# An FFT filter and a squared-ReLU FFN in one kernel: W_in loaded in seven pieces, a reordered opening, two FFT stages one slot later, and x cast on GpSimd

## The chip, the cores and the metric

The kernel runs on one core of a Trainium2 chip. A core has five engines with queues of their own: TensorE (PE in the profile; its weight loads are PEld), VectorE (DVE), ScalarE (ACT), GpSimd (POOL) and SyncE (SP), which here only issues DMAs. TensorE reads the on-chip memory SBUF and writes the accumulator memory PSUM; VectorE and ScalarE copy results from PSUM to SBUF. The metric is the device time of one execution in microseconds (us). Before the change the median of 13 runs is 796.56 us, from 794.07 to 798.56.

## The reference

```python
def _attn_ref(x, filt_r, filt_i):              # x: (8, 3008, 256), filters: (1505, 256)
    X = np.fft.rfft(x, axis=1)
    F = (filt_r + 1j * filt_i)[None, :, :]
    Y = X * F
    return np.fft.irfft(Y, n=x.shape[1], axis=1).astype(np.float32)

def _moe_ref(x, w_in, w_out):                  # x: (24064, 256), w_in: (256, 2048), w_out: (2048, 256)
    h = np.maximum(x @ w_in, 0.0)
    return (h * h @ w_out).astype(np.float32)

out = _moe_ref(attn_out.reshape(8 * 3008, 256), w_in, w_out)
```

Each batch of x is filtered along its 3008 positions by a real FFT, a product with a complex filter, and the inverse transform. The 24064 rows that come out go through a two-layer FFN whose hidden values are rectified and squared. Inputs and output are float32; inside, the kernel works in float16 with float32 accumulation.

## The kernel before, in words

**The FFT as matmuls.** 3008 is 64 x 47, and the transform of a batch is done in four stages of matmuls with constant matrices. Stage A (`unit_a`; `chunk_a0` and `chunk_a` for batches 0 and 1) transforms along 47 and gives u. For batches 1 to 7, u is written to the DRAM buffer dU (`write_u`) and read back in another layout as ut (`read_u`); for batch 0 it is turned on TensorE (`turn_u`). Stage B (`unit_b`, 12 units a batch) transforms along 64 into psB; VectorE multiplies that by the filter sF (L451, "prod"), makes a swapped copy in two halves (L458, L459), and `unit_s` adds (L465). Stage P (`unit_p`, `unit_p0` for batch 0) goes back along 64, ScalarE copies the result to ze, and ze is written to the DRAM buffer dZ. `read_z` reads dZ back as four z tiles, and stage Y (`unit_y`, 16 units) goes back along 47; its result yt is copied by ScalarE (even units) or VectorE (odd units).

**The FFN.** 47 groups of 512 rows. `ffn_g1` (L560) makes 2 of 16 hidden tiles in one call, ScalarE rectifies them (L564), `ffn_sq` squares them on VectorE (L568), and `ffn_g2` (L577) multiplies by W_out; ScalarE copies the output (L588) and SyncE writes it.

**Slots.** All is unrolled, in an order written out by hand. The main loop at the end of the kernel runs over slots, 8 to a group: in each, g1 of the present group, the FFT units planned for "place 0", g2 of the group before, the units for "place 1", the output, and the square. `fft_plan(b)` puts each unit of batch b at a slot counted from a start of its own: slot 48 is that of the first group which needs rows of batch b (slot 40 for batch 1). Loads and casts of the next batch's x (`load_x`, `cast_x`) are in the plan too. Engines work through their own queues in program order; a DMA is issued by SyncE once what it waits for is done, and one that waits holds those behind it. Each engine waits for another only where data or a buffer demands it.

**Buffers.** A tile pool with a tag has so many buffers, and a new tile waits until the last use of the tile that had its buffer. Of the 32-bit tiles "x32" (1 MB) there are two; the opening uses them in turn for x of batch 0, for the two halves of W_in, and for x of batch 1. PSUM has two buffers each of psF, psO and psH; in the main loop stages A, B, P and Y share the two psF, g1 has psH and g2 has psO.

**The opening** (all before the main loop). It loads x of batch 0 as three tiles (`load_wide`), the filters (`load_f`), the constants, W_in and x of batch 1; casts them to float16 (`cast_wide`, `cast_win`, L680, L695); runs stage A of batch 0 and the turns; and spreads the filter into sF by small selection matmuls (`place_f(im, k)`: im is 0 for the real and 1 for the imaginary part, k counts groups of four columns; each call has about 0.87 us of matmuls and one copy of 1024 elements, L303 on ScalarE or L307 on VectorE). `sSPx` is a copy of the stage-P constants with the halves of the partitions swapped, made on GpSimd. Then a loop of seven rounds runs stages B and P of batch 0 with the rest of `place_f` between them:

```python
for k in range(7):
    if k < 6:
        unit_b(0, 2 * k)
        if k < 5:
            place_f(1, k + 1, nc.scalar)
        unit_b(0, 2 * k + 1)
    if k > 0:
        unit_p0(k - 1)
    if k < 2:
        place_f(0, k + 4, nc.scalar)
    if k in (1, 2):
        load_wide(1, k - 1)
        cast_wide(1, k - 1, nc.gpsimd, nc.gpsimd)
```

After it come the first reads of z and the load of W_out, stage A of batch 1 (`chunk_a`, lines 378 and 380), four Y units of batch 0, and slot 0. The product of unit p in stage B needs both `place_f(0, p // 2)` and `place_f(1, p // 2)`.

Of the kernel before, what the change touches and what calls it, by code (L numbers as in the profile page):

```python
# [110 lines left out]
def kernel(  # L111
# [96 lines left out]
    sPF = p_out.tile([128, 6, 128], F16, tag="ost", name="sPF")  # L208

    xw32, xw16 = {}, {}  # L210
    halves, later = ((0, 0), (0, 1)), []

    def load_wide(b, k):

        v0 = xrows[b * S:b * S + 2048, :].rearrange("(p m) d -> p m d", m=16)
        v1 = xrows[b * S + 2048:b * S + 3072, :].rearrange("(p m) d -> p m d", m=8)
        pool, tag = (p_x32, "x32") if k < 2 else (p_y, "yt") if b else (p_h2, "h2")
        t = pool.tile([128, 8, D], F32, tag=tag, name=f"xw_{b}_{k}")
        v = (v0[:, 0:8, :], v1, v0[:, 8:16, :])[k]
        for m in (slice(0, 4), slice(4, 8)) if (b, k) in halves else (slice(0, 8),):  # L220
            if m.stop > 4 and m.start == 4:
                later.append((t, v, m))
            else:
                nc.sync.dma_start(out=t[:, m, :], in_=v[:, m, :])
        xw32[(b, k)] = t

    def cast_wide(b, k, *engs, parts=(0, 1)):
        if 0 in parts:
            xw16[(b, k)] = p_x16.tile([128, 8, D], F16, tag="x16", name=f"xw16_{b}_{k}")
        for i in parts:  # L230
            m = slice(4 * i, 4 * i + 4)
            engs[i].tensor_copy(out=xw16[(b, k)][:, m, :], in_=xw32[(b, k)][:, m, :])
# [42 lines left out]

    f16s = []

    def place_f(im, k, eng, rotate=False):

        if rotate:  # L280
            banks, groups = bank_pair(f"psf_{im}_{k}")
        else:
            t = psH(f"psf_{im}_{k}")
            banks, groups = [t[:, 0, :], t[:, 1, :]], [(t, 0)]
        for i in range(4):
            c = 4 * k + i
            e0, e1 = D * c, D * (47 - c)
            cuts = [0] + [d for d in range(1, D)
                          if (e0 + d) % QF == 0 or (c and (e1 + d) % QF == 0)] + [D]
            for d0, d1 in zip(cuts, cuts[1:]):  # L290
                o = banks[i // 2][:, (i % 2) * D + d0:(i % 2) * D + d1]
                q, a = divmod(e0 + d0, QF)
                nc.tensor.matmul(o, sPF[:, PQ.index((0, q)), :], f16s[0][:, im, a:a + d1 - d0],  # L293
                                 start=True, stop=False)
                q, a = divmod(e1 + d0, QF) if c else (0, QF + d0)
                nc.tensor.matmul(o, sPF[:, PQ.index((1, q)), :], f16s[0][:, im, a:a + d1 - d0],  # L296
                                 start=False, stop=True)
        for t, i in groups:
            n = t.shape[1]
            dst = sF[:, im, 4 * k + 2 * i:4 * k + 2 * i + 2 * n, :]  # L300
# [21 lines left out]
    def load_wout(k):  # L322
        if k == 0:
# [9 lines left out]

    x16s, us, uts, prods, zes, zts, yts = {}, {}, {}, {}, {}, {}, {}

    def cast_x(b, c, eng=nc.vector):
        t = p_x16.tile([94, 8, D], F16, tag="x16", name=f"x16_{b}_{c}")
        eng.tensor_copy(out=t, in_=x32s.pop((b, c))[0:94])  # L338
        x16s[(b, c)] = t
# [49 lines left out]
                else:  # L389
                    eng.tensor_copy(out=o, in_=pv)  # L390

    def chunk_a0(c, ks):

        for k in ks:
# [213 lines left out]
    def fft_plan(b):  # L608
# [24 lines left out]
        if b + 1 < B:  # L633
            for c in range(2):
                put(t0 - 13, 1, load_x, b + 1, c)
            for c in range(4):
                r = t0 - 8 + 3 * c
                put(r, 1, cast_x, b + 1, c)
                if c < 2:
                    put(r, 1, load_x, b + 1, c + 2)  # L640
        for n in range(16):
            if b == 1:
                put(38 + n // 2 if n > 3 else 39, n % 2, unit_y, b, n)
            else:
                put(44 + n // 2, n % 2, unit_y, b, n)
        return plan

    def run(plan, r, place):
# [2 lines left out]


    uT = p_h2.tile([128, 2, NC, 128], F16, tag="h2", name="uT")
    for i in range(2):
        for k in range(2):
            cast_wide(0, k, nc.vector, nc.vector, parts=(i,))
    cast_wide(0, 2, nc.vector, nc.gpsimd)

    def load_const(t, d, k):
        c = slice(12 * k, 12 * k + 12)  # L660
# [11 lines left out]
    for k in range(2):  # L672
        for c in (1, 3):
            chunk_a0(c, (k,))
    f16s.append(p_h2.tile([128, 2, QF + D], F16, tag="h2", name="f16"))
    e0, e1 = slice(0, 1504), slice(1504, QF)
    for im in range(2):
        nc.gpsimd.tensor_copy(out=f16s[0][:, im, QF:], in_=nyq[:, im, :])
    for im, e in ((0, e0), (0, e1), (1, e0)):
        nc.gpsimd.tensor_copy(out=f16s[0][:, im, e], in_=f32s[im][:, e])  # L680
    for k in range(2):
        sSPx.append(p_u.tile([128, 12, 128], F16, tag="u", name=f"sSPx_{k}"))
        c = slice(12 * k, 12 * k + 12)
        nc.gpsimd.tensor_copy(out=sSPx[k][0:64], in_=sSP[64:128, c, :])
        nc.gpsimd.tensor_copy(out=sSPx[k][64:128], in_=sSP[0:64, c, :])
    for k in range(2):
        cast_win(k)
    uts[0] = p_ut.tile([128, NC, D], F16, tag="ut", name="ut_0")
# [24 lines left out]
    read_z(0, 1)  # L713
# [59 lines left out]
```

## Time and profile before

| what | value |
|---|---|
| median of 13 runs | 796.56 us (794.07 to 798.56) |
| the profiled execution | 796.39 us; span of its instructions 794.6 us |
| granted TensorE clock, mean | 0.997 |
| TensorE busy (PE) | 781.4 us, 98% of the span |
| VectorE, ScalarE, GpSimd busy | 552.4, 554.5 and 24.2 us |
| chain that ended last | PE 91%, DMA 5%, DVE 1%, ACT 1% |
| DMA | 107.32 MB, mean 135 GB/s |

The page follows one execution. A group line names the source line, the engine, the operation, out<-in, the shape and the count, then the group's busy time and the mean of one in ns, then the engine's idle time just before and who ended it. A timeline line gives the start and the length in us, the engine, the line, and the count of merged instructions; in square brackets stands the idle time before it and what ended it. Matmuls are pipelined, so the shown length of one is longer than the distance to the next: holes in TensorE are best read from the distances between starts.

### The profile page before, as it was taken

The page shows a single profiled execution, that of the slowest core. Times are in us where ns is not written, and L with a number is a line of the kernel's source. Part 1 is how long each engine was busy: PE and PEld are TensorE (multiplying, and loading weights), DVE is VectorE, ACT ScalarE, POOL GpSimd, SP SyncE. Part 2 cuts the span into 40 slices and gives each one's busy share as a digit, 9 for nine tenths or more (in the row PEclk, how much of TensorE's full clock was granted, in tenths as well). Part 3 has the DMA queues.
Part 4 walks back from the last instruction along what each step waited for, and adds up shares of the span by engine and source line. Part 5 has one row for each costly group of instructions (what it writes and reads, how often), then busy time and mean ns, then how long its engine had stood idle before and what let it go on. Part 6 is the DMA issues. An engine that isn't in the chain of part 4 may idle for free.

```text
span 794.6 us, 14801 instructions
## 1 busy us (share of the span) xinstructions
PE 781.4 (98%) x6102; PEld 553.1 (70%) x6102; DVE 552.4 (70%) x898; ACT 554.5 (70%) x708; POOL 24.2 (3%) x27
## 2 busy tenths in 40 slices
PE   8989999999999999999999999999999999999998
PEld 6746667667676667867677677776777667776666
DVE  6956995589755897559965699557995589554342
ACT  3866776767767676767777677676777767766664
POOL 3710000000000000000000000000000000000000
PEclk9999999999999999999999999999999999999999
DMA  9994554346714567155462555424663342511111
GB/s 350 369 272 137 149 148 126 90 138 165 204 42 111 163 159 179 41 172 148 125 168 59 162 153 149 117 73 154 155 177 91 90 141 80 125 45 41 40 41 54
DMA packets 88139, 107.32 MB, mean 135 GB/s; under 512 B 6288, under 2 KB 78864, under 8 KB 83856
## 3 DMA queue, kind: packets, MB, share of 16 engines
q1 hardware_dynamic: 87864, 106.19, 46.6%
q8 instruction: 48, 0.79, 0.4%
q10 hardware_dynamic: 144, 0.18, 0.1%
q14 instruction: 19, 0.16, 0.1%
q0 software_dynamic: 64, 0.00, 0.0%
HBM read 58.12 MB, written 48.23 MB: 134 GB/s over the span
## 4 chain that ended last, share of the span: by engine, by line
PE 91%; DMA 5%; DVE 1%; ACT 1%; SPq 0%; issue 0%; POOL 0%; ACTq 0%; DVEq 0%; POOLq 0%
PE psO L577 40%; PE psH L560 39%; PE psA L359 3%; PE psY L530 3%; PE psB L443 2%; PE psP L494 2%; DMA xw<-in_x_dram 2%; DMA ut<-dU 1%; DMA zt<-dZ 1%; PE psf L293 1%; ACT h L564 1%; PE psf L296 1%; ACT sF L303 0%; DMA dU<-u 0%; PE psT L420 0%; DMA dZ<-ze 0%
## 5 line engine op out<-in xcount | busy, mean ns | idle before, releaser
L564 ACT ACTIVATE h<-psH 128x1024 f16<-128x1024 f32 x376 | 384.9, 1024 | 190.4 <-PE psH L560 188.6
L577 PE MATMUL psO<-sWout,h 128*128 128x256 f16 x3008 | 388.6, 272 | 0.0
L560 PE MATMUL psH<-yt,sWin 128*128 128x512 f16 (+7 forms) x1728 | 386.9, 351 | 1.8 <-DVE yt L539 0.8
L577 PEld LDWEIGHTS <-h 128*128 128x128 f16 x3008 | 290.6, 98 | 77.2
L568 DVE TENSOR_TENSOR h<-h 128x1024 f16<-128x1024 f16 x376 | 253.8, 685 | 100.7 <-ACT h L564 99.2
L560 PEld LDWEIGHTS <-sWin 128*128 128x128 f16 x1728 | 159.5, 98 | 101.7 <-issue 3.5
L451 DVE TENSOR_TENSOR prod<-psB,sF 128x1024 f16<-128x1024 f32 x84 | 102.5, 1220 | 6.3 <-PE psB L443 6.0
L539 DVE CAST yt<-psY 128x376 f16<-128x376 f32 x62 | 34.0, 549 | 57.4 <-PE psY L530 57.4
L365 DVE CAST u<-psA 96x512 f16<-96x512 f32 x50 | 34.3, 687 | 47.3 <-PE psA L359 45.1
L496 ACT CAST ze<-psP 128x512 f16<-128x512 f32 x84 | 49.2, 585 | 17.9 <-PE psP L494 16.0
L588 ACT COPY ost<-psO 128x512 f32<-128x512 f32 (+1 forms) x96 | 55.8, 581 | 6.7 <-PE psO L577 5.3
L530 PEld LDWEIGHTS <-zt 112*128 112x128 f16 x512 | 34.8, 98 | 12.2 <-issue 2.3
L530 PE MATMUL psY<-sC,zt 112*128 112x94 f16 x512 | 42.3, 205 | 0.6 <-ACT yt L537 0.3
L465 DVE TENSOR_TENSOR yf<-prod,yf 128x512 f16<-128x512 f16 x84 | 35.7, 425 | 2.9
L443 PE MATMUL psB<-ut,sSB 128*128 128x256 f16 x192 | 36.5, 272 | 0.7 <-DMA ut<-dU 0.4
L359 PE MATMUL psA<-x,sC 94*96 94x512 f16 x96 | 36.6, 382 | 0.0
L443 PEld LDWEIGHTS <-sSB 128*128 128x128 f16 x192 | 18.6, 98 | 21.3 <-issue 2.2
L494 PE MATMUL psP<-yf,sSP 128*128 128x256 f16 x168 | 32.1, 273 | 0.2 <-ACT yt L537 0.2
L537 ACT CAST yt<-psY 128x376 f16<-128x376 f32 x66 | 30.8, 468 | 1.1 <-PE psY L530 0.6
L338 DVE CAST x<-x 94x2048 f16<-94x2048 f32 x24 | 29.2, 1216 | 0.0
L363 ACT CAST u<-psA 96x512 f16<-96x512 f32 x50 | 28.6, 572 | 0.0
L458 DVE COPY yf<-prod 64x512 f16<-64x512 f16 x84 | 24.3, 289 | 2.9
(63 smaller groups left out, 252.9 us busy)
## 6 DMA issues: line engine op xcount, KB each, us to landing
x<-in_x_dram SPq DMA_DIRECT2D x20, 768.0 KB
zt<-dZ SPq DMA_DIRECT2D x64, 192.0 KB
dU<-u SPq DMA_DIRECT2D x28, 384.0 KB
dZ<-ze SPq DMA_DIRECT2D x28, 384.0 KB
out_dram<-ost SPq DMA_DIRECT2D x66, 128.0 KB
out_dram<-ost SPq DMA_DIRECT2D x31, 256.0 KB
ut<-dU SPq DMA_DIRECT2D x7, 1024.0 KB
xw<-in_x_dram SPq DMA_DIRECT2D x4, 1024.0 KB
```

The source lines that it names most:

```text
L359: nc.tensor.matmul(ps[0:96, :], sSA, x16s[(b, c)][:, m, :], start=True, stop=True)
L443: nc.tensor.matmul(ps[:, i * D:(i + 1) * D], sSB[:, 2 * p + i, :], uts[b][:, 2 * p + i, :], start=True, stop=True)
L451: nc.vector.tensor_mul(out=prod, in0=ps.rearrange("p (a d) -> p a d", d=D).unsqueeze(1).to_broadcast([128, 2, 2, D]), in1=sF[:, :, 2 * p:2 ...
L465: nc.vector.tensor_add(out=yf, in0=prod[:, 0], in1=yf)
L494: nc.tensor.matmul(ps[:, i * D:(i + 1) * D], sSP[:, 2 * p + i, :], yf[:, i, :], start=True, stop=True)
L496: nc.scalar.copy(out=zes[(b, c)][:, 2 * i6:2 * i6 + 2, :], in_=ps.rearrange("p (a d) -> p a d", d=D))
L530: nc.tensor.matmul(ps[:, 94 * jj:94 * jj + 94], zt[:, 4 * (g % 2) + jj, dt * 128:(dt + 1) * 128], sSY, start=True, stop=True)
L560: nc.tensor.matmul(ps[:, i, o:o + n], sWin[:, dt, jt * 128:(jt + 1) * 128], yts[b][:, dt, r:r + n], start=(dt == 0), stop=(dt == 1))
L564: nc.scalar.activation(out=h2[:, 2 * s:2 * s + 2, :], in_=ps, func=AF.Relu)
L568: nc.vector.tensor_mul(out=v, in0=v, in1=v)
L577: nc.tensor.matmul(pso[g][:, t % 2, :], h2s[g][:, jt, t * 128:(t + 1) * 128], sWout[:, jt, :], start=(jt == 0), stop=(jt == NJT - 1))
L588: nc.scalar.copy(out=ost[:, h0:h0 + step, :], in_=pso[g][:, h0:h0 + step, :])
```

## The change

Three parts, done together.

- The opening. x of batch 0 is loaded in three whole tiles instead of the first two in halves. W_in is loaded in seven pieces into buffers of the tags ze, prod and yf, not into the two x32 buffers, and cast on GpSimd piece by piece. All three loads of batch 1's x are issued right after W_in's. The imaginary filter is cast in three parts on VectorE, GpSimd and ScalarE. `place_f(0, 2)` and `place_f(0, 3)` move from before the loop into it, and `place_f(1, 0)` may be split over two engines (it gets a PSUM tile of one piece, so ScalarE copies all of it). The sSPx copies are made in twelve pieces of 512 elements instead of four of 1536. The third x tile of batch 1 is cast on VectorE and ScalarE after the loop, no longer on GpSimd before it; the other two are cast on GpSimd after W_in.
- The plan. In batches 2 to 7, stage B begins at slot 19 (was 18) and ends at slot 37 as before, and Y takes slots 45 to 52 (was 44 to 51). In batch 1, stage B ends at slot 31 (was 32), z is read at slot 34 (was 35), and Y takes two units a slot from slot 38 (before, its first four units stood in slot 39). The loads of batch 2's x come one slot sooner.
- The x casts of batches 2 to 7 go from VectorE to GpSimd, one slot sooner in the plan (two in batch 1's); the loads of the third and fourth x tile are issued two slots after the cast whose buffer they take, not in its slot.

```diff
-    halves, later = ((0, 0), (0, 1)), []
...
-        for m in (slice(0, 4), slice(4, 8)) if (b, k) in halves else (slice(0, 8),):
-            if m.stop > 4 and m.start == 4:
-                later.append((t, v, m))
-            else:
-                nc.sync.dma_start(out=t[:, m, :], in_=v[:, m, :])
+        nc.sync.dma_start(out=t, in_=(v0[:, 0:8, :], v1, v0[:, 8:16, :])[k])
...
-    for k in range(2):
+    for k in range(3):
         load_wide(0, k)
-    for t, v, m in later:
-        nc.sync.dma_start(out=t[:, m, :], in_=v[:, m, :])
-    load_wide(0, 2)
...
-    def load_win(k):
-        w32s[k] = p_x32.tile([128, DFF], F32, tag="x32", name=f"win32_{k}")
-        nc.sync.dma_start(out=w32s[k], in_=moe_w_in[128 * k:128 * k + 128, :])
-
-    def cast_win(k):
-        for j in range(2):
-            c = slice(1024 * j, 1024 * j + 1024)
-            nc.gpsimd.tensor_copy(out=sWin[:, k, c], in_=w32s[k][:, c])
+    def load_win():
+
+        for k, c, n, pool, tag in ((0, 0, 768, p_ze, "ze"), (0, 768, 768, p_ze, "ze"),
+                                   (0, 1536, 512, p_prod, "prod"), (1, 0, 768, p_ze, "ze"),
+                                   (1, 768, 512, p_prod, "prod"), (1, 1280, 512, p_prod, "prod"),
+                                   (1, 1792, 256, p_yf, "yf")):
+            t = pool.tile([128, n], F32, tag=tag, name=f"win32_{k}_{c}")
+            nc.sync.dma_start(out=t, in_=moe_w_in[128 * k:128 * k + 128, c:c + n])
+            wins.append((t, k, slice(c, c + n)))
+
+    def cast_win():
+        for t, k, c in wins:
+            nc.gpsimd.tensor_copy(out=sWin[:, k, c], in_=t)
...
-    def cast_x(b, c, eng=nc.vector):
+    def cast_x(b, c, eng=nc.gpsimd):
...
-        t0 = 14 if b == 1 else 18
+        t0 = 14 if b == 1 else 19
         for p in range(12):
-            r = t0 + (18 if b == 1 else 19) * p // 11
+            r = t0 + (17 if b == 1 else 18) * p // 11
...
-        t0 = 35 if b == 1 else 40
+        t0 = 34 if b == 1 else 40
...
             for c in range(4):
-                r = t0 - 8 + 3 * c
+                r = t0 - 9 + 3 * c
                 put(r, 1, cast_x, b + 1, c)
                 if c < 2:
-                    put(r, 1, load_x, b + 1, c + 2)
+                    put(r + 2, 1, load_x, b + 1, c + 2)
         for n in range(16):
-            if b == 1:
-                put(38 + n // 2 if n > 3 else 39, n % 2, unit_y, b, n)
-            else:
-                put(44 + n // 2, n % 2, unit_y, b, n)
+            put((38 if b == 1 else 45) + n // 2, n % 2, unit_y, b, n)
...
-    for k in range(2):
-        load_win(k)
-    for k in range(2):
-        for c in (0, 2):
-            chunk_a0(c, (k,))
-    for k in range(2):
-        for c in (1, 3):
-            chunk_a0(c, (k,))
+    load_win()
+    for k in range(3):
+        load_wide(1, k)
+    for c in (0, 2, 1, 3):
+        chunk_a0(c)
...
-    for im, e in ((0, e0), (0, e1), (1, e0)):
-        nc.gpsimd.tensor_copy(out=f16s[0][:, im, e], in_=f32s[im][:, e])
+    for e in (e0, e1):
+        nc.gpsimd.tensor_copy(out=f16s[0][:, 0, e], in_=f32s[0][:, e])
+    uts[0] = p_ut.tile([128, NC, D], F16, tag="ut", name="ut_0")
+    turn_u(0, nc.scalar)
+    turn_u(1, nc.vector)
+    turn_u(2, nc.scalar)
+    turn_u(3, nc.vector)
+    place_f(0, 0, nc.scalar, rotate=True)
+    for eng, e in ((nc.vector, slice(0, 1024)), (nc.gpsimd, slice(1024, 2048)),
+                   (nc.scalar, slice(2048, QF))):
+        cast(eng, f16s[0][:, 1, e], f32s[1][:, e])
+    turn_u(4, nc.vector)
+    place_f(0, 1, nc.scalar, rotate=True)
+    turn_u(5, nc.vector)
+    place_f(1, 0, nc.scalar, nc.vector, rotate=True)
+    for k in range(6):
+        if k % 3 == 0:
+            sSPx.append(p_u.tile([128, 12, 128], F16, tag="u", name=f"sSPx_{k}"))
+        c, o = slice(4 * k, 4 * k + 4), slice(4 * k % 12, 4 * k % 12 + 4)
+        nc.gpsimd.tensor_copy(out=sSPx[-1][0:64, o, :], in_=sSP[64:128, c, :])
+        nc.gpsimd.tensor_copy(out=sSPx[-1][64:128, o, :], in_=sSP[0:64, c, :])
+    cast_win()
     for k in range(2):
...
-    load_wide(1, 2)
-    cast_wide(1, 2, nc.gpsimd, nc.gpsimd)
-    for k in range(6):
-        turn_u(k, nc.vector if k in (1, 3, 4, 5) else nc.scalar)
-        if k > 2:
-            place_f(0, k - 3, nc.scalar, True)
-    nc.vector.tensor_copy(out=f16s[0][:, 1, e1], in_=f32s[1][:, e1])
-    place_f(0, 3, nc.vector, True)
-    place_f(1, 0, nc.scalar)
+        cast_wide(1, k, nc.gpsimd, nc.gpsimd)
...
-        if k < 2:
-            place_f(0, k + 4, nc.scalar)
-        if k in (1, 2):
-            load_wide(1, k - 1)
-            cast_wide(1, k - 1, nc.gpsimd, nc.gpsimd)
+        if k < 4:
+            place_f(0, k + 2, nc.scalar)
+    cast_wide(1, 2, nc.vector, nc.scalar)
     read_z(0, 0)
```

More of the change, by code (lines that the diff above doesn't have):

```diff
@@ L218, in load_wide, with cast, cast_wide @@
         t = pool.tile([128, 8, D], F32, tag=tag, name=f"xw_{b}_{k}")
-        v = (v0[:, 0:8, :], v1, v0[:, 8:16, :])[k]
-        for m in (slice(0, 4), slice(4, 8)) if (b, k) in halves else (slice(0, 8),):
-            if m.stop > 4 and m.start == 4:
-                later.append((t, v, m))
-            else:
-                nc.sync.dma_start(out=t[:, m, :], in_=v[:, m, :])
-        xw32[(b, k)] = t
[L227 to L230, printed above, removed]
+        nc.sync.dma_start(out=t, in_=(v0[:, 0:8, :], v1, v0[:, 8:16, :])[k])
+        xw32[(b, k)] = t
+    def cast(eng, out, in_):
+        (eng.copy if eng is nc.scalar else eng.tensor_copy)(out=out, in_=in_)
+    def cast_wide(b, k, *engs):
+        t = p_x16.tile([128, 8, D], F16, tag="x16", name=f"xw16_{b}_{k}")
+        for i in range(2):
             m = slice(4 * i, 4 * i + 4)
-            engs[i].tensor_copy(out=xw16[(b, k)][:, m, :], in_=xw32[(b, k)][:, m, :])
-    for k in range(2):
+            cast(engs[i], t[:, m, :], xw32[(b, k)][:, m, :])
+        xw16[(b, k)] = t
+    for k in range(3):
         load_wide(0, k)
-    for t, v, m in later:
-        nc.sync.dma_start(out=t[:, m, :], in_=v[:, m, :])
-    load_wide(0, 2)
     f32s = []
@@ L276, with place_f @@
     f16s = []
-    def place_f(im, k, eng, rotate=False):
+    def place_f(im, k, *engs, rotate=False):
         if rotate:
@@ L299, in place_f @@
             n = t.shape[1]
+            eng = engs[i % len(engs)]
             dst = sF[:, im, 4 * k + 2 * i:4 * k + 2 * i + 2 * n, :]
@@ L311 @@
     w32s = {}
[L313 to L320 removed]
+    def load_win():
[9 more added lines that the diff above has]
+            nc.gpsimd.tensor_copy(out=sWin[:, k, c], in_=t)
+    wins = []
     def load_wout(k):
@@ L390, in chunk_a, with chunk_a0 @@
                     eng.tensor_copy(out=o, in_=pv)
-    def chunk_a0(c, ks):
-        for k in ks:
+    def chunk_a0(c):
+        for k in range(2):
             banks, groups = bank_pair(f"psA_0_{c}_{k}")
@@ L653 @@
     uT = p_h2.tile([128, 2, NC, 128], F16, tag="h2", name="uT")
-    for i in range(2):
-        for k in range(2):
-            cast_wide(0, k, nc.vector, nc.vector, parts=(i,))
-    cast_wide(0, 2, nc.vector, nc.gpsimd)
+    for k in range(3):
+        cast_wide(0, k, nc.vector, nc.gpsimd if k == 2 else nc.vector)
     def load_const(t, d, k):
@@ L666 @@
         load_const(sSP[:, c, :], dSP, k)
-    for k in range(2):
-        load_win(k)
-    for k in range(2):
-        for c in (0, 2):
-            chunk_a0(c, (k,))
-    for k in range(2):
-        for c in (1, 3):
-            chunk_a0(c, (k,))
+    load_win()
+    for k in range(3):
+        load_wide(1, k)
+    for c in (0, 2, 1, 3):
+        chunk_a0(c)
     f16s.append(p_h2.tile([128, 2, QF + D], F16, tag="h2", name="f16"))
@@ L678 @@
         nc.gpsimd.tensor_copy(out=f16s[0][:, im, QF:], in_=nyq[:, im, :])
-    for im, e in ((0, e0), (0, e1), (1, e0)):
-        nc.gpsimd.tensor_copy(out=f16s[0][:, im, e], in_=f32s[im][:, e])
-    for k in range(2):
[L682 to L688, printed above, removed]
-    load_wide(1, 2)
-    cast_wide(1, 2, nc.gpsimd, nc.gpsimd)
-    for k in range(6):
-        turn_u(k, nc.vector if k in (1, 3, 4, 5) else nc.scalar)
-        if k > 2:
-            place_f(0, k - 3, nc.scalar, True)
-    nc.vector.tensor_copy(out=f16s[0][:, 1, e1], in_=f32s[1][:, e1])
-    place_f(0, 3, nc.vector, True)
-    place_f(1, 0, nc.scalar)
+    for e in (e0, e1):
[20 more added lines that the diff above has]
+    cast_win()
+    for k in range(2):
+        cast_wide(1, k, nc.gpsimd, nc.gpsimd)
     for k in range(7):
```

## The prediction

> **What bounds the kernel now.** I read the page's shares first (TensorE busy 98% of 794.6 us), then busy time by stretch, the chain that ended last, single engines' timelines around each hole, and the queue's own waits. From about 61 us on, TensorE is the bound: slot after slot its matmuls follow each other, eight of L577 or four of L560 starting 0.87 us apart, so only holes there can be won. The first 61 us are different. Busy time by stretch; columns are stretch, length, then PE, PEld, DVE, ACT and POOL busy (instructions), granted clock, DMA share, GB/s:
>
> ```profile
> 30.00:40.00 10.00, 9.06 (x85) 7.68 (x84) 9.23 (x9) 8.35 (x8) 7.39 (x8) 1.00 0.90 310
> 40.00:50.00 10.00, 7.83 (x39) 4.24 (x38) 3.73 (x5) 4.63 (x7) 2.02 (x2) 0.83 0.86 248
> 50.00:60.00 10.00, 9.14 (x62) 4.47 (x59) 7.02 (x13) 7.93 (x12) 0.00 (x0) 1.00 1.09 293
> ```
>
> The stretch 40 to 50 us has an idle TensorE, a lowered clock (0.83) and no other busy engine. The chain of waits there (start, length, what) says why:
>
> ```profile
> 33.72 7.42 DMA xw<-in_x_dram
> ...
> 41.26 1.05 POOL xw L232
> ...
> 42.35 0.38 PE psA L380
> ...
> 43.26 0.43 PE psA L378
> ```
>
> Batch 1's second x tile is fetched only from 33.72 us, because it waits for a buffer that W_in holds; GpSimd casts it at 41.26 and stage A of batch 1 starts 2.04 us late. Then eight matmuls run at 0.43 us instead of 0.217: 1.7 us more, and the stage ends at 49.0 instead of 45.2 (39.94 + 24 x 0.217). In the steady part the holes are small. TensorE's timeline around the two kinds:
>
> ```profile
> 257.82 0.59 PE L560 MATMUL psH<-yt,sWin 128*128 128x512 f16 x2
> 258.25 1.04 PE L577 MATMUL psO<-sWout,h 128*128 128x256 f16 x8
> 259.13 1.03 PE L560 MATMUL psH<-yt,sWin 128*128 128x512 f16 x4
> 260.56 0.38 PE L443 MATMUL psB<-ut,sSB 128*128 128x256 f16 x2 [0.40 <-DMA ut<-dU]
> ```
> ```profile
> 500.30 1.03 PE L560 MATMUL psH<-yt,sWin 128*128 128x512 f16 x4
> 501.58 0.33 PE L530 MATMUL psY<-sC,zt 112*128 112x94 f16 x4 [0.26 <-DMA zt<-dZ]
> ...
> 125.82 0.70 PE L530 MATMUL psY<-sC,zt 112*128 112x94 f16 x8 [0.26 <-ACT yt L537]
> ```
>
> 259.13 + 0.87 is 260.00, so stage B lost 0.56 us there. The same sum at the first stage-B matmul of the other batches gives 0.26 (164.9), 0.18 (355.7), 0.15 (450.8) and 0.28 (546.4); at 501.58 it gives 0.41 for stage Y. Slot 39 of batch 1, with four Y units on two PSUM banks, lost 0.43 + 0.22 us at 125.8 to 126.2, and 0.47 at 127.24 (stage 1 of the FFN waiting for the last y).
>
> The casts that move, from the page's groups and GpSimd's timeline:
>
> ```profile
> L338 DVE CAST x<-x 94x2048 f16<-94x2048 f32 x24 | 29.2, 1216 | 0.0
> ```
> ```profile
> 12.00 1.56 POOL L232 CAST xw<-xw 128x1024 f16<-128x1024 f32 x1 [9.34 <-DMA xw<-in_x_dram]
> 33.35 2.02 POOL L232 CAST xw<-xw 128x1024 f16<-128x1024 f32 x2
> ```
>
> [...] the GpSimd cast at 12.00 took 1.56 us instead of 1.03, the 0.5 being the rest of a 0.69 us VectorE cast begun at 11.97. Nothing here shows GpSimd beside L568, which has two SBUF inputs. [...]
>
> **The change, part by part.** *Opening loads.* x of batch 0 comes whole, not in halves. Stage A of batch 0 then starts at about 10.2 us rather than 9.62. Free: VectorE can't begin copying its results before the third x tile's cast (11.97 to 12.6), and its eight copies end at 16.57 either way. Without that cover it would cost 0.6.
>
> *W_in in seven pieces.* The pieces lie in buffers that batch 1's stages use later, so both x32 buffers are free at 11 us and all three batch-1 loads are queued before any dZ write. The same bytes at the 425 GB/s of 20 to 30 us put the last of them near 38 us, not 41.1. GpSimd's row grows: 1034 ns at 1024 and 1441 at 1504 elements give 0.17 us + 0.85 ns an element; 12 sSPx copies of 512 make 7.2 us (4 took 5.85), W_in 4.6 (was 4.0), two x tiles 4.1. From the sSP landing (23.3 us) it ends near 39.3, its first half of each x tile by 38.3. Stage A then needs no wait, if it starts after that.
>
> *Filter order.* Cutting the filt_i cast over three engines lets place_f(1,0) start at about 21.95 us (filt_i in at 20.9, ScalarE's 960 elements 0.96), not 23.18: ScalarE's copy of it starts at 23.0, not 24.27. But 15 ScalarE copies follow instead of 13, since place_f(0,2) and (0,3) move into the loop. Before, eleven of them from 24.27 to 36.68 took 1.128 us each. place_f(1,5) is number 12: 23.0 + 12 x 1.128 + 1.11 = 37.65. Two products of 1.2 us and half a P unit end at 40.5, the last ze at 41.5 (41.15 before). So the loop ends 0.35 us later, although it began 1.27 us sooner. Stage A of batch 1 then runs 40.5 to 45.7 at full clock (24 x 0.217). The third x tile's cast, now on VectorE and ScalarE after the loop, costs these 0.7 and 1.0 us, hidden: its use comes 3.5 us into stage A.
>
> *What is late next.* Stage Y of batch 0 needs dZ written and read back. Before, the last ze ended at 41.15, the second read was issued at 44.13, landed at 47.5, and Y began at 49.15, after stage A. Now: 41.5 + 2.5 (a write with no backlog; 2.94 before, with one) + 0.1 + 2.9 (the earlier read half's landing) = 47.0. Gain 2.1 us (0.3 to 3.2, the upper end being stage A's own end). It is carried to 61 us only if W_out keeps up: that is queued behind the z reads at about the same 44.1 us and lands at 56.3, and its second half's casts come at about 58.7. The z tile for Y unit 4 lands at 52.8; that unit comes at 54.1. Both fit.
>
> *B and Y one slot later* (about 2 us): takes the five stage-B waits, 1.4, and the 0.41 of Y; FFN needs its first y at slot 48 and n = 0 to 3 are done in slots 45 and 46. The last P, its dZ write and the reads of z stay at slots 39 and 40; the first P's and their dZ writes move one slot with B, and no one waits for them singly. In batch 1 B, P, dZ and z reads end one slot sooner and Y starts one sooner, so the four slots between read and use remain; so does its x load, one slot sooner in SyncE's queue. Batch 1's two-per-slot Y takes 0.65; the 0.47 at 127.24 stays, since unit 3 still stands directly before slot 40. Sum 2.45 (1.2 to 2.5; DMA landings vary).
>
> *x casts on GpSimd.* 24 x 1.22 = 29.2 us leave VectorE. A cast of 2048 is 1.9 us on GpSimd, and the order on SyncE's queue improves: x loads 3 and 4, issued two slots after the cast, no longer hold that queue (44.1 us in 10 waits, all behind transfers with slack). They run when their data land, the first two close together near slots 30 and 32. [...] it loses 0.7 to 1.9 us per cast and gains 1.2: about even in sum, but in clumps. The place that feels it is psF: two buffers, and where stage B has units in two consecutive slots, the next unit waits for the product before; the trace leaves about 0.5 us there. A 1.9 us delay can thus cost 1.4 us; none of it if the cast meets products or idle time. Bounds per stage 0 to 1.4; I take 0.2 for each of six stages, 1.3 in all.
>
> **Sum** against the profiled execution's own 796.39 us: -2.1 - 2.45 + 1.3 = -3.3, so 793.1; the median shown is 796.56, 0.2 above it: 793.3.
>
> **Rivals.** (1) [...] each of six B stages loses the full 1.4 us, 8.4 together: 796.6 - 4.55 + 8.4 = 800.4, slower. For: VectorE is 37.8 of 40 us busy from 260 to 300. Against: 1.2 us per cast is freed. It turns the sign from 4.55 + 1.6 = 6.2 us, 1.0 per stage. (2) *The opening gives nothing*: the loop's 15 copies run at 1.2 us, or the clock drops once more in the 1.3 us that TensorE waits for z, and Y starts at 49.1. Then 796.6 - 2.45 + 1.3 = 795.4. For: 0.35 us of the loop is already lost. (3) [...] everything else holding, and stage A's end sets Y: 796.6 - 3.2 - 2.45 = 790.9.
>
> **Numbers.** A measurement of this kernel tells about 0.2% (1.6 us) from no change: 795.0 to 798.2 counts as same. Forecast 0.44 (own range 791.5 to 795.0), rival 3 0.12, both faster: 0.56. Rival 2[...], 0.20: same. Rival 1, with its milder forms above 798.2, 0.24. The range takes in rival 3 and rival 1's milder half: 790.7 to 799.
>
> **What would show it.** Right: no TensorE hole before L380's stage and clock near 1.0 from 40 to 50 us; Y's first matmul near 47; the loop's last ze near 41.5; W_in casts ending near 35; first stage-B matmuls without a DMA wait; L568 and L458 rows longer than 685 and 289 ns where GpSimd casts[...] with psB waiting for L451's product less than 0.3 us a stage. Wrong: psB or psP waits on VectorE above 1 us per stage; Y's first matmul at 49 or later; stage A waiting for GpSimd; DVE or ACT late in slots 4 to 7 for W_out.

## The result, and the profile after

The changed kernel takes 805.3 us (median of 7 runs, 803.67 to 807.12), the kernel before 796.55 us (32 runs) beside it: ratio 1.0112, 95% interval 1.0098 to 1.0126. It is slower by 8.75 us where 3.3 us less was forecast. The profiled execution, 803.67 us with a span of 801.9, is the fastest of the seven. In the changed file the numbers move by two below the opening: L560 is L562, L577 is L579, L568 is L570, L443 is L445, L451 is L453, L458 is L460, L465 is L467, L338 is L340.

The opening first. Busy time by stretch after, with the columns of the table shown of before:

```profile
30.00:40.00 10.00, 9.22 (x84) 7.62 (x83) 8.06 (x8) 9.17 (x9) 8.93 (x12) 1.00 0.87 325
40.00:50.00 10.00, 7.79 (x54) 4.71 (x54) 5.68 (x8) 5.94 (x9) 0.00 (x0) 1.00 0.75 215
50.00:60.00 10.00, 9.65 (x48) 4.28 (x47) 5.95 (x10) 7.77 (x10) 0.00 (x0) 0.83 1.09 300
```

The clock is full from 40 to 50 us (1.00), as forecast, but TensorE is no busier there (7.79 us against 7.83), and the lowered clock (0.83) now stands in the next stretch. GpSimd's timeline, and after it the chain of waits (start, length, what), say why ("..." marks lines left out, here and below):

```profile
30.69 4.38 POOL L320 CAST sWin<-win 128x768 f16<-128x768 f32 x7
35.03 3.98 POOL L222 CAST xw<-xw 128x1024 f16<-128x1024 f32 x4
```
```profile
40.95 1.02 ACT ze L484
...
41.99 2.37 DMA dZ<-ze
...
44.49 3.41 DMA zt<-dZ
...
48.04 0.33 PE psY L532 x4
```

W_in is cast by 35.07 and x of batch 1 by 39.01; the last ze ends at 41.97. Then stage Y waits for z until 48.04.

In the steady part the DMA waits ahead of stages B and Y are gone, as forecast. TensorE's timeline at the two places shown of before:

```profile
263.58 1.03 PE L562 MATMUL psH<-yt,sWin 128*128 128x512 f16 x4
264.45 0.38 PE L445 MATMUL psB<-ut,sSB 128*128 128x256 f16 x2
...
508.27 1.03 PE L562 MATMUL psH<-yt,sWin 128*128 128x512 f16 x4
509.14 0.33 PE L532 MATMUL psY<-sC,zt 112*128 112x94 f16 x4
```

Each starts 0.87 us after the four matmuls before it: no hole. But new holes have come. TensorE's waits after (engine, line, for whom; us in total, times, longest):

```profile
PE psB L445 <- DVE prod L453: 4.4, 6, 1.1
PE psP L496 <- DVE yf L467: 1.7, 2, 1.2
```

And in the chain that ended last, VectorE holds a quarter where it held 1%:

```profile
PE 70%; DVE 25%; DMA 3%; ACT 1%; issue 1%; SPq 0%; DVEq 0%; ACTq 0%
```

The groups point to the cause (busy us, mean ns of one, idle before), first those of before:

```profile
L568 DVE TENSOR_TENSOR h<-h 128x1024 f16<-128x1024 f16 x376 | 253.8, 685 | 100.7 <-ACT h L564 99.2
L465 DVE TENSOR_TENSOR yf<-prod,yf 128x512 f16<-128x512 f16 x84 | 35.7, 425 | 2.9
L458 DVE COPY yf<-prod 64x512 f16<-64x512 f16 x84 | 24.3, 289 | 2.9
```
```profile
L570 DVE TENSOR_TENSOR h<-h 128x1024 f16<-128x1024 f16 x376 | 270.8, 734 | 113.9 <-ACT h L566 113.7
L340 POOL CAST x<-x 94x2048 f16<-94x2048 f32 x24 | 49.4, 2056 | 511.0 <-DMA x<-in_x_dram 487.9
L467 DVE TENSOR_TENSOR yf<-prod,yf 128x512 f16<-128x512 f16 x84 | 37.4, 445 | 2.9
L460 DVE COPY yf<-prod 64x512 f16<-64x512 f16 x84 | 31.9, 380 | 2.9
```

Squares went from 685 ns to 734, adds from 425 to 445, copies (L460) from 289 to 380. The product L453 is unchanged (1218 ns, 1220 before). VectorE gave up 29.2 us of casts and is as busy as before (552.6 us, 552.4). Two places show what a mean hides. The first, in the timeline of GpSimd, VectorE and TensorE (ScalarE and the matmuls of other stages left out):

```profile
284.35 1.89 POOL L340 CAST x<-x 94x2048 f16<-94x2048 f32 x1 [71.15 <-DMA x<-in_x_dram]
284.85 1.53 DVE L460 COPY yf<-prod 64x512 f16<-64x512 f16 x1
286.40 0.29 DVE L461 COPY yf<-prod 64x512 f16<-64x512 f16 x1
286.61 1.04 PE L579 MATMUL psO<-sWout,h 128*128 128x256 f16 x8
286.64 1.89 POOL L340 CAST x<-x 94x2048 f16<-94x2048 f32 x1 [0.40 <-PE psH L562]
286.72 2.08 DVE L467 TENSOR_TENSOR yf<-prod,yf 128x512 f16<-128x512 f16 x1
...
288.86 0.39 PE L496 MATMUL psP<-yf,sSP 128*128 128x256 f16 x2 [1.22 <-DVE yf L467]
```

The first cast ends at 286.24, and the copy beside it ends 0.14 us later, 1.24 us longer than its 0.29. The second ends at 288.53; the add beside it ends at 288.80 and took 2.08 us instead of 0.42. TensorE's stage P waits for that add: 288.86 - 286.61 - 0.87 = 1.38 us. A later stage-B unit, which needs a product that stands behind all this in VectorE's queue, is late at 294.62 by another 0.75 us.

The second place is the stage B of the batch before:

```profile
189.26 1.89 POOL L340 CAST x<-x 94x2048 f16<-94x2048 f32 x1 [0.78 <-DMA x<-in_x_dram]
189.30 3.00 DVE L570 TENSOR_TENSOR h<-h 128x1024 f16<-128x1024 f16 x2
192.22 1.21 DVE L453 TENSOR_TENSOR prod<-psB,sF 128x1024 f16<-128x1024 f32 x1
...
196.91 0.38 PE L445 MATMUL psB<-ut,sSB 128*128 128x256 f16 x2 [1.08 <-DVE prod L453]
```

Here it is two squares that the cast holds: 3.00 us where a pair without a cast takes 1.28. The product behind them starts late, and the stage-B unit at 196.91 is 1.24 us late. The same stands in two more of the six stages (pairs of squares of 2.98 us at 479.06 and 575.71, holes of 1.24 us at 486.64 and 583.30). So copies, adds and squares alike cost time when a product stands behind them. From 62 us on the changed kernel's VectorE-made holes at stages B and P add up to 7.8 us in that execution (distances between starts).

### The profile page after: what moved, and what is told of

Same layout as the page of the kernel before. It is cut to its first block, busy times and chain, and to the rows that moved or that the text cites. A ratio compares the mean times of both kernels' runs of the same rounds, so it can differ in the third digit from the quotient of the medians.

```text
span 801.9 us, 14863 instructions
## 1 busy us (share of the span) xinstructions
PE 782.3 (98%) x6102; PEld 552.0 (69%) x6102; DVE 552.6 (69%) x873; ACT 557.6 (70%) x711; POOL 73.0 (9%) x60
## 4 chain that ended last, share of the span: by engine, by line
PE 70%; DVE 25%; DMA 3%; ACT 1%; issue 1%; SPq 0%; DVEq 0%; ACTq 0%
PE psO L579 31%; PE psH L562 30%; DVE prod L453 8%; DVE h L570 7%; DVE yf L467 3%; DVE yf L460 3%; PE psA L361 3%; PE psY L532 3%; DVE yf L461 2%; DMA f<-in_filt_i_dram 2%; PE psB L445 1%; PE psP L496 1%; PE psf L287 1%; PE psf L290 1%; DMA zt<-dZ 0%
## 5 line engine op out<-in xcount | busy, mean ns | idle before, releaser
L579 PE MATMUL psO<-sWout,h 128*128 128x256 f16 x3008 | 388.8, 272 | 1.1 <-DVE h L570 1.1
L562 PE MATMUL psH<-yt,sWin 128*128 128x512 f16 (+7 forms) x1728 | 388.4, 352 | 1.3 <-DVE yt L541 0.7
L570 DVE TENSOR_TENSOR h<-h 128x1024 f16<-128x1024 f16 x376 | 270.8, 734 | 113.9 <-ACT h L566 113.7
L579 PEld LDWEIGHTS <-h 128*128 128x128 f16 x3008 | 290.5, 98 | 79.7 <-DVE h L570 1.4
L562 PEld LDWEIGHTS <-sWin 128*128 128x128 f16 x1728 | 159.9, 98 | 102.5 <-issue 5.1
L453 DVE TENSOR_TENSOR prod<-psB,sF 128x1024 f16<-128x1024 f32 x84 | 102.3, 1218 | 1.5 <-PE psB L445 1.4
L340 POOL CAST x<-x 94x2048 f16<-94x2048 f32 x24 | 49.4, 2056 | 511.0 <-DMA x<-in_x_dram 487.9
L445 PE MATMUL psB<-ut,sSB 128*128 128x256 f16 x192 | 36.4, 272 | 4.5 <-DVE prod L453 4.4
L467 DVE TENSOR_TENSOR yf<-prod,yf 128x512 f16<-128x512 f16 x84 | 37.4, 445 | 2.9
L445 PEld LDWEIGHTS <-sSB 128*128 128x128 f16 x192 | 18.4, 98 | 25.7 <-issue 7.6
L460 DVE COPY yf<-prod 64x512 f16<-64x512 f16 x84 | 31.9, 380 | 2.9
```

The costliest lines, as they stand in the source:

```text
L445: nc.tensor.matmul(ps[:, i * D:(i + 1) * D], sSB[:, 2 * p + i, :], uts[b][:, 2 * p + i, :], start=True, stop=True)
L453: nc.vector.tensor_mul(out=prod, in0=ps.rearrange("p (a d) -> p a d", d=D).unsqueeze(1).to_broadcast([128, 2, 2, D]), in1=sF[:, :, 2 * p:2 ...
L460: nc.vector.tensor_copy(out=yf[0:64], in_=prod[64:128, 1])
L467: nc.vector.tensor_add(out=yf, in0=prod[:, 0], in1=yf)
L562: nc.tensor.matmul(ps[:, i, o:o + n], sWin[:, dt, jt * 128:(jt + 1) * 128], yts[b][:, dt, r:r + n], start=(dt == 0), stop=(dt == 1))
L570: nc.vector.tensor_mul(out=v, in0=v, in1=v)
```

## The experiments

The theory: a copy, an add or a square of VectorE that starts while GpSimd casts x ends only after the cast (so do 24 of the 25 in the changed kernel's trace, and none of the three products there does); the stage-B chain of product, two copies and an add runs late in VectorE's queue, and TensorE waits at psB and psP. Rival A: the opening or the plan is at fault, and the longer rows are bystanders. Rival B: GpSimd is merely too slow, so that x comes late (no stage-A wait on GpSimd stands in the trace, which speaks against it; a run below, with the casts later still, settles it).

**One part at a time.** First the changed kernel with only the x casts back on VectorE.

```diff
-    def cast_x(b, c, eng=nc.gpsimd):
+    def cast_x(b, c, eng=nc.vector):
```

> The changed kernel with one word undone: the x casts of batches 2 to 7 are back on VectorE, at the changed slots. [...] (a GpSimd cast of 1.9 us holds off VectorE's yf copies, adds and squares, and TensorE then waits for a product or a yf), the 9.9 us of TensorE holes that the changed kernel's trace shows between 90 and 590 us go, and what the plan saves stays: 794 to 796 us, ratio to the kernel before 0.996 to 1.000, no psP or psB wait on VectorE above 0.3 us. If the later stage B and Y or the denser stage B of batch 1 are the cause, the engine of the cast doesn't matter: 803 us or more.

Measured: 796.35 us (13 runs), ratio to the kernel before 1.0008 [0.9999, 1.0016]. So 1.0112/1.0008, or 8.3 us, is GpSimd's. The two profiled executions say where: TensorE's holes from 62 to 790 us (distances between starts) add up to 10.9 us in the changed kernel and to 4.5 here, and slot 8 is reached at 60.79 and at 59.32 us, the former behind the lowered clock of 50 to 60 us. That is 6.4 + 1.5 of the 7.9 us between the two spans. So in that execution, the fastest of the seven, the holes show 6.4 us of what the ratio puts at 8.3.

But this kernel isn't at the forecast 793 either. Its wait at stage B:

```profile
PE psB L445 <- DVE prod L453: 1.1, 5, 0.2
```

Five stages of B lose some 0.38 us each by distances between starts, and stage 2 of the FFN waits 1.23 us for a square at 114.4, in batch 1.

The converse: the kernel before, with nothing but its casts on GpSimd.

```diff
-    def cast_x(b, c, eng=nc.vector):
+    def cast_x(b, c, eng=nc.gpsimd):
```

> The kernel before with one word changed: its x casts on GpSimd, slots and opening as before. [...] VectorE loses up to 1.9 us a cast in the same stages B, and the kernel before pays for it as well: 803 to 807 us, ratio 1.008 to 1.013. If the loss needs the later stage B: within 0.2% of the kernel before (795 to 798 us).

Measured: 808.88 us (5 runs), ratio 1.0166 [1.0145, 1.0186]. The loss is larger, 13.2 us, 2.2 a stage. Its timeline of GpSimd, VectorE and TensorE in one stage (other lines between these left out):

```profile
284.95 3.92 POOL L338 CAST x<-x 94x2048 f16<-94x2048 f32 x2 [76.14 <-PE psP L494]
285.07 1.92 DVE L458 COPY yf<-prod 64x512 f16<-64x512 f16 x1
287.00 2.02 DVE L459 COPY yf<-prod 64x512 f16<-64x512 f16 x1
...
291.87 0.38 PE L443 MATMUL psB<-ut,sSB 128*128 128x256 f16 x2 [1.08 <-DVE prod L451]
```

Its waits for the product at psB are 8.6 us, 4.4 in the changed kernel. Two casts run in a row, and both copies of one unit held. Neither the opening nor the plan is needed for the loss.

Then the kernel before with only the new slots of B and Y (part of the edit is shown), and the kernel before with only the new opening, which is the changed kernel with its plan and its casts put back.

```diff
-        t0 = 14 if b == 1 else 18
+        t0 = 14 if b == 1 else 19
...
+            put((38 if b == 1 else 45) + n // 2, n % 2, unit_y, b, n)
```

> The kernel before with the slots of stages B and Y alone changed (batches 2 to 7 one later; batch 1 denser, Y two units a slot); the x casts stay on VectorE. The removed DMA waits (1.4 us before stage B, 0.4 before Y) and the batch 1 Y unit waits (0.65) make 2.4 us: 794.2 us, ratio 0.997. If the plan is the cause of the loss: 800 us or more.

> The changed kernel's opening with the plan and the VectorE casts of the kernel before. The changed kernel's trace reaches slot 8 at 60.8 us where the kernel before does at 61.0, since Y of batch 0 waited for z until 48.0 and the next eight matmuls ran at half clock: 796.4 us, ratio 0.999 to 1.001. If the opening is worth what was forecast: 794.5. If it costs later (x or W_out late): 798 or more.

Measured: slots alone 794.02 us (16 runs), 0.9977 [0.9965, 0.9988]; opening alone 795.97 us (13 runs), 1.0001 [0.9992, 1.0011]. The slots give 1.8 us by the ratio, 2.0 between medians, of the 2.45 forecast; the opening gives nothing. TensorE's first Y and the first FFN matmuls after it, in the run with the old opening:

```profile
47.67 0.33 PE L530 MATMUL psY<-sC,zt 112*128 112x94 f16 x4
...
49.41 0.78 PE L560 MATMUL psH<-yt,sWin 128*128 128x512 f16 x2 [0.24 <-ACT yt L537]
```

and with the new one:

```profile
48.03 0.33 PE L532 MATMUL psY<-sC,zt 112*128 112x94 f16 x4 [1.31 <-DMA zt<-dZ]
...
49.49 2.03 PE L562 MATMUL psH<-yt,sWin 128*128 128x512 f16 x8 [0.28 <-ACT yt L539]
```

The old opening, with a 1.57 us wait for GpSimd still in it but a full clock, reaches the FFN no later. What the profiled execution of the kernel before had lost was the halved clock; this one did not have it, and of the 37 executions of the kernel before beside these runs 18 show a mean clock of 1.000. The execution with the new opening then has a hole of 1.34 us at 641.1, where stage B of batch 7 waits for ut; the kernel before has none there, and where it comes from stays open.

**What of the opening waits for z.** The opening alone, with the first of batch 0's four z tiles read from a constant instead of from dZ; so part of batch 0's output is not computed, and that read waits for no write.

```diff
+            if b == 0 and c == 0:
+                nc.sync.dma_start(out=zt[64 * k:64 * k + 32], in_=w)
...
+                continue
```

> The opening alone (plan and casts of the kernel before), and the first z tile of batch 0 read from a constant of the same size instead of from dZ, so that stage Y of batch 0 no longer waits for the writes of stage P; its values for 2 of 8 row blocks of batch 0 are left out of the computation. If that wait is what swallows the opening's gain: Y's first matmul at about 46.5 us instead of 48.0, slot 8 at about 58 instead of 59.5, and 794.5 us. If the first slots were bound by something else (W_out, ScalarE), the time stays within 0.1% of 796.

Measured: 795.33 us (22 runs), 0.9989 [0.998, 0.9998]. TensorE's first Y:

```profile
46.75 0.33 PE L538 MATMUL psY<-sC,zt 112*128 112x94 f16 x4
```

Y starts 1.28 us sooner, the next z tile then makes unit 4 wait at 54.06 (0.37 us), and slot 8 is reached at 58.58 us instead of 59.53. So the z chain takes about 1 us of the opening's gain in the trace; the intervals of the two ratios overlap, so the times alone don't show it.

**Where the cast falls.** Each cast of the changed kernel in four pieces of 512 elements:

```diff
-        eng.tensor_copy(out=t, in_=x32s.pop((b, c))[0:94])
+        for i in range(4):
+            eng.tensor_copy(out=t[:, 2 * i:2 * i + 2, :], in_=x32[0:94, 2 * i:2 * i + 2, :])
```

> The changed kernel, each GpSimd cast of 2048 elements made in four of 512 (about 0.6 us each), nothing else moved. [...] VectorE waits at most 0.6 us at a time[...], so the holes shrink to about what the psF margin leaves (0.5 us): 796 to 800 us. If what counts is the total time that GpSimd reads SBUF ([...]some 50 us in 24 casts, more in pieces): 804 us or more.

Measured: 798.72 us (22 runs), 1.0031 [1.0021, 1.0041]. Most of the loss is gone, but the waits for the product remain (4.3 us in 6), and squares, adds and copies (L462 here) still take 709, 451 and 325 ns in the mean, against 685, 425 and 289 before.

And the casts left whole on GpSimd, but loaded and placed after the last P unit, before and beside Y, where VectorE has no copies and adds to make:

```diff
-                put(t0 - 13, 1, load_x, b + 1, c)
+                put(t0 - 4 + c, 1, load_x, b + 1, c)
...
-                r = t0 - 9 + 3 * c
+                r = t0 + (0, 1, 4, 5)[c]
...
-                    put(r + 2, 1, load_x, b + 1, c + 2)
+                    put(r + 1, 1, load_x, b + 1, c + 2)
```

> The changed kernel with GpSimd casts of 2048 as they are, but with x loaded later, so that they fall between the last P unit and Y (slots 40 to 45; in batch 1 from slot 34 on). There VectorE has one square a slot and TensorE waits for none of it within 2 us. [...] the casts still stretch squares in the trace, but the holes go, as do the late casts of VectorE: 793.5 to 796 us. If a GpSimd cast costs wherever it runs: 803 us or more.

Measured: 792.9 us (10 runs, 792.68 to 793.23), 0.996 [0.9945, 0.9974]. It beats both kernels. Its groups:

```profile
L570 DVE TENSOR_TENSOR h<-h 128x1024 f16<-128x1024 f16 x376 | 272.7, 735 | 117.7 <-ACT h L566 114.4
L467 DVE TENSOR_TENSOR yf<-prod,yf 128x512 f16<-128x512 f16 x84 | 35.7, 425 | 2.9
L460 DVE COPY yf<-prod 64x512 f16<-64x512 f16 x84 | 24.3, 289 | 2.9
```

The squares lose as much as in the changed kernel (735 and 734 ns), some 19 us in all (272.7 against 253.8), and no psB wait is left. The copies and adds lose nothing, since none runs there. So lost VectorE time costs nothing by itself: squares held in these slots have no product behind them, while in the changed kernel squares as well as copies and adds were held ahead of one. The casts run still later here than in the changed kernel, which also settles rival B. With the casts the loads of x moved too, and the casts were not tried on VectorE in these slots; so what of the gain over the kernel before comes from which of these is not shown.

**Reading or writing.** To see whether a GpSimd instruction that only writes holds the adds and squares as the cast does: the changed kernel with x cast on VectorE, and on GpSimd, ahead of each cast, a copy of two elements (so that the fills wait for x to land) and two fills of the whole tile.

```diff
+        nc.gpsimd.tensor_copy(out=t[:, 0, 0:2], in_=x32[0:94, 0, 0:2])
+        for _ in range(2):
+            nc.gpsimd.memset(t, 0.0)
```

> The changed kernel with the x casts on VectorE, and on GpSimd, as soon as an x tile has landed, a two-element copy and two memsets of the float16 tile (writes that read no SBUF; the cast overwrites them). [...] the squares (685 ns) and adds (425 ns) keep their length beside a memset, while the copies of L460 and L461[...] may be held for the memset's length. If GpSimd holds everything: squares of over 1 us as in the changed kernel. The time is that of the casts on VectorE plus whatever is held: 796 to 801.

Measured: 823.35 us, one run. The groups, and the timeline where a copy, an add and a square meet fills:

```profile
L574 DVE TENSOR_TENSOR h<-h 128x1024 f16<-128x1024 f16 x376 | 252.0, 684 | 94.5 <-ACT h L570 94.1
L471 DVE TENSOR_TENSOR yf<-prod,yf 128x512 f16<-128x512 f16 x84 | 35.7, 425 | 2.9
L464 DVE COPY yf<-prod 64x512 f16<-64x512 f16 x84 | 35.4, 421 | 2.9
```
```profile
292.36 3.69 POOL L343 MEMSET x<- 94x2048 f16 x2
292.74 1.56 DVE L464 COPY yf<-prod 64x512 f16<-64x512 f16 x1
...
296.23 0.42 DVE L471 TENSOR_TENSOR yf<-prod,yf 128x512 f16<-128x512 f16 x1
296.29 1.80 POOL L343 MEMSET x<- 94x2048 f16 x1
296.57 0.68 DVE L574 TENSOR_TENSOR h<-h 128x1024 f16<-128x1024 f16 x1
```

Beside fills, squares and adds keep their 684 and 425 ns; copies are held (421 ns in the mean, 1.56 us here). Beside the changed kernel's casts all three took longer (734, 445 and 380 ns). The time missed its forecast by far. One reason is the experiment's own: VectorE's cast must wait for the fills of its tile (15.2 us), and everything behind it in the queue with it. Another is that the fills are twice as many as the changed kernel's casts and hold more copies (35.4 us for L464, 31.9 in the changed kernel). The run does not separate the two.

**The rest of the gap.** The slots alone give 0.9977, slots and opening with VectorE's casts one slot sooner (and the loads of the third and fourth x tile two slots after them) 1.0008. Two runs were to show that these casts make the difference, with batch 1's moved after its stage B:

```diff
-                r = t0 - 8 + 3 * c
+                r = (32, 33, 36, 37)[c] if b == 1 else t0 - 8 + 3 * c
```

the first on the slots alone, the second on opening and slots, there also with one filter copy of the loop on VectorE.

> The kernel before with the B and Y slots of the change and VectorE's x casts where they stood, but those of batch 1 after its stage B (slots 32, 33, 36, 37 in place of 26, 29, 32, 35), so that VectorE has its squares of batch 1's dense stage B to itself. If the 0.75 us wait of FFN stage 2 for a square at 113.9 us in the run with the slots alone comes from those casts: 793.3 us (794.0 - 0.75), no hole above 0.5 us between 62 and 790 us. If it comes from stage B's products alone, the hole stays and the time is 794.0 us.

> The changed kernel's opening and its B and Y slots, with x cast on VectorE in the slots of before (not one sooner; batch 1 after its stage B), and one filter copy of the loop on VectorE instead of ScalarE. If it was the casts one slot sooner, beside two stage-B units in consecutive slots, that cost the run with all on VectorE its 2.3 us against the slots alone, then this one stands at 793.5 us (792.5 to 794.5), with no psB waits on VectorE above 0.3 us in all. If the opening itself carries a cost into the steady part, it stays near 796.3 us, with those waits still there.

Measured: 798.81 us (13 runs), 1.0035 [1.0015, 1.0054], and 798.8 us (6 runs), 1.004 [1.0025, 1.0056]: both slower, not as expected of either cause. The holes in the steady part are gone, the one at 113.9 us too, but a new wait stands in batch 1. TensorE's waits and SyncE's timeline in the first of the two:

```profile
PE psY L530 <- DMA zt<-dZ: 3.5, 1, 3.5
```
```profile
114.48 0.32 SPq L192 DMA_DIRECT2D x<-in_x_dram  x1
...
116.27 0.49 SPq L192 DMA_DIRECT2D x<-in_x_dram  x1
116.86 8.26 SPq L512 DMA_DIRECT2D zt<-dZ  x8
```

The loads of the third and fourth x tile follow the first two casts, and so moved too: now directly ahead of the reads of z, whose issue takes 8.26 us instead of the 5.68 in the run with the slots alone. Only the last two casts were therefore moved, (26, 29, 36, 37), in both.

> As the run whose batch-1 casts all came after stage B, but only the last two do (slots 26, 29, 36, 37), so that the x loads that follow the first two casts are issued at slots 26 and 29 again, ahead of the z reads by five slots. If those late loads alone held back the z reads (3.7 us of wait at 126.5 us and a halved clock after it), the wait is gone, the hole at 113.9 us stays away, and the time is 793.3 us. If the casts at slots 36 and 37 are to blame, it stays near 798.8 us.

> The same placing of the casts with the changed kernel's opening. No psB wait on VectorE above 0.3 us in all, no wait for z in batch 1: 793.5 us (792.5 to 794.5) if the run with all casts on VectorE stood at 796.35 us only for its casts one slot sooner; near 796.3 us if the opening carries a cost into the steady part.

Measured: 794.71 us (6 runs), 0.9972 [0.9959, 0.9985], and 794.71 us (9 runs), 0.998 [0.9968, 0.9991]. The z wait is gone, so the loads made it. The 0.76 us hole at 115 us is back, so it goes with the first two casts, not with the third as I had expected. And opening plus slots, with the casts made in batches 2 to 6 in their old places, stand where the slots alone do. 0.998 against 1.0008, intervals apart, puts the price of one slot sooner on VectorE at 2.2 us.

That price is rather too low, because the run behind 0.998 carries a cost of its own. The filter copy that it has on VectorE makes TensorE wait in the opening, a wait that the run with the casts back on VectorE doesn't have:

```profile
PE psP L482 <- ACT sF L298: 1.0, 1, 1.0
```

Its last ze ends at 43.29 us instead of 42.10, and it reaches slot 8 at 60.78 instead of 59.32, both at full clock. From 62 us on TensorE's holes add up to 2.0 us in it and to 4.5 in the other, 2.5 us apart, and none at stage B is left.

## Why the prediction was wrong, point by point

Three steps of ratios lead from the kernel before to the changed one: opening and slots together 0.998, which is -1.6 us; casts one slot sooner, still on VectorE, from there to 1.0008, +2.2; casts on GpSimd from there to 1.0112, +8.3. Together 8.9 us, the 1.0112 itself, as quotients of one another must. The first of these runs also has batch 1's last two casts later and the costly filter copy on VectorE. Without it, from the slots alone (0.9977) and the opening alone (1.0001), the first step is -1.8 and the second 2.4.

- *x casts on GpSimd* is the step that failed. It named squares and copies that take longer beside GpSimd's casts, the even balance of VectorE's time in sum, and the waits that would betray it (psB and psP on VectorE), and all of that is in the trace (734 and 380 ns, 552.6 us against 552.4, 4.4 and 1.7 us). Its loss of 0.7 to 1.9 us per cast was an estimate of the author's: before, no GpSimd instruction runs beside L458, L465 or L568. It was priced at 0.2 us for each of six stages (1.3 in its sum, though six times 0.2 is 1.2); 8.3/6 = 1.4 was measured in the mean, its own upper bound and rival 1's price. The choice of 0.2 rested on a cast meeting products (they do keep their length, 1.21 to 1.23 us in all 84) or idle time, and on a freed 1.2 us per cast. But TensorE doesn't wait for VectorE's sum over a stage. It waits for one product and one add at a time, through an in-order queue. The first two casts of a stage run when their data land, one soon after the other. In the first place shown they hold a copy and an add of one unit: 1.24 + 1.66 = 2.9 us late, against a margin of about 0.5; in three other stages the second lengthens a pair of squares ahead of a product by 1.7 us. Nor is 1.4 a bound for one stage: 1.38 and 0.75 stand in the same one. The time of the casts that left VectorE was freed elsewhere in its queue.
- *Casts one slot sooner.* The prediction worked this out only for SyncE's queue. With the casts on VectorE the same slots cost 2.2 to 2.5 us. The changed kernel's own trace can't show this share, since no cast is on VectorE there.
- *Filter order* was right to half a microsecond: last ze at 41.97, forecast 41.5. *W_in in seven pieces* was right: casts ended at 35.07 and 39.01 (forecast near 35 and 39.3), and stage A waited for nothing. *Opening loads* left no mark in the sum (stage A of batch 0 starts at 9.74, forecast 10.2).
- *What is late next* was right in naming z and wrong in its worth. Write 2.37 us (2.5 assumed), read 3.41 (2.9 assumed), so Y at 48.04 instead of 47.0. And the 2.1 us were counted from 49.15 of one profiled execution with a halved clock; in another, without it, the old opening starts Y at 47.67. The gain was a lowered clock taken for a fixed cost. From 43.05 to 46.4 us the first of the two has 3.35 us at a clock of 0.51, after a wait of 2.04 us; what lowers the clock, the runs do not show. Rival 2, "the opening gives nothing", held in its outcome. It expected Y at 49.1 us, which came at 48.04. Of its two reasons, the loop's copies did not slow down (last ze at 41.97); the clock did drop after the 1.33 us wait for z in the changed kernel's profiled execution (0.50 from 50 to 53 us), but not in that of the opening alone (1.31 us of wait, mean clock 1.000), which gains nothing either.
- *B and Y one slot later* was right: 1.8 us by the ratio against 2.45, inside its 1.2 to 2.5, and the DMA waits are gone. The denser stage B of batch 1 was taken as free; its 0.75 us wait for a square (at 113.9 in the run with the slots alone) and 0.44 us before stage P (at 93.6) were not seen coming.
- Both rivals came true together: 796.55 - 1.6 + 2.2 + 8.3 = 805.45. The range reached only to half of rival 1 with the other gains intact, so it could not hold 805.3.

## What to carry to other kernels

When work moves to GpSimd, don't add up VectorE's freed and lost time: list which VectorE instructions stand in the slots where the cast will run, and follow each through VectorE's queue to the matmul that waits for it or for what stands behind it. The same 24 casts cost 8.3 us in the slots of stage B, where copies, adds and squares stand ahead of products, and nothing that shows in the slots after it, beside squares with slack. Move a cast and its buffer's next load moves along, so look at what that load now stands ahead of; and before counting a halved clock as a gain, see whether every execution has it.

## What the runs showed of the hardware

- Squares held alike (734 and 735 ns) stand in kernels of 805.3 and 792.9 us. GpSimd casts of about 1.9 us lengthened copies to as much as 2.02 us (kernel before with its casts on GpSimd), adds to 2.08 and pairs of squares to 3.00 (changed kernel), and left the product at 1218 ns. GpSimd's fills lengthened copies (421 ns in the mean) and left adds and squares alone (425 and 684 ns).
- Cutting the casts into pieces of 512 gave back 6.4 us of the 8.3 (1.0112 to 1.0031), though GpSimd then worked longer (71.0 us in 96 pieces, against 49.4 in 24).
- After a wait of TensorE a lowered clock stood in one execution and not in another. In the profiled execution of the first run with the late x loads, a 3.55 us wait that ends at 126.5 us goes with a clock of 0.75 from 120 to 130 us and 0.91 from 130 to 140; in that of the second, with a wait of 3.70 us, the clock there is 1.00. Executions of the first with a mean granted clock of 1.000 took 795.68 to 796.04 us, and those with 0.991 took 801.9 to 802.76: the same program, the same chip.
